# Two copies ahead of two subtractions in a weight fold, and another order of the last projection tiles

## The chip, the cores and the metric

The kernel runs on one core of one Trainium2 chip. The metric is the device time of one execution in microseconds (us), as the median of several runs. A profiled execution stands beside them; its trace gives each instruction's start and duration, and the views of the profile are made from it. Engines are named as the profile does: PE is TensorE (PEld its weight loads), DVE is VectorE, ACT is ScalarE, POOL is GpSimd, SP is SyncE, which issues most transfers.

## What is computed

The reference adds a linear attention with a learned feature map and a two-layer MLP to the input `x` (2048 tokens of width 640, 32 heads of 20, hidden width 1728), both on the layer-normalized input:

```python
xn = layernorm(x)
# attention
qkv = (xn @ wqkv)                       # split into q, k, v per head
pq, pk = q @ w_phi, k @ w_phi           # 20x20 per head
phi_q = concat(softmax(pq), softmax(-pq))
phi_k = concat(softmax(pk), softmax(-pk))
kv  = phi_k^T @ v                       # summed over all tokens, per head
z   = sum over tokens of phi_k
o   = (phi_q @ kv) / (phi_q @ z + 1e-6)
A   = o @ wo
# MLP, on layernorm(xn)
B   = gelu(layernorm(xn) @ w1 + b1) @ w2 + b2
out = x + A + B
```

All of it is float32. The kernel splits each float32 operand into a high and a low part of a shorter format and makes three matmuls of each product (`mm3`, lines 63 to 66: high x high, high x low, low x high). So most of what ACT, DVE and POOL do is such splitting: the high part is a copy, the low part a subtraction of that copy from the source (`split`, lines 51 to 61).

## The kernel before

**Stages.** The tokens lie in four blocks of 512. First PE does the MLP for blocks 0 and 1: 14 chunks of the hidden width in groups `g` of two, for each group and block a first half (width 640 to hidden, five steps of three matmuls for each of two chunks) and a second half (hidden to width, five banks). Then comes the projection of all 16 token tiles of 128 to features and values (`proj`, lines 594 to 603), then the MLP for blocks 2 and 3 with the attention beside it, then the output projection.

**Work beside the MLP.** `mlp.beside` (lines 248 and 290) is a generator that PE's loop moves one step on after every three matmuls. In groups 1 and up for blocks 0 and 1 it is `prep` (line 483): it folds `w_phi` into the key and query weights, makes the statistics of blocks 2 and 3, splits the value weights, and makes the normalized input of blocks 2 and 3.

**The fold.** `prep_fold` (lines 445 to 468) runs for keys and queries and six groups of heads, 12 times. Each time it makes two pieces: four chunks of the width and then one. For a piece, PE makes four matmuls or one into one PSUM bank (line 459; the trace has two entries for each). Of a head's 19 columns 16 go to one place (the main part, `dst`) and 3 to another (the rest, columns from `c3` of `wkv_`). Both are split: copies on ACT (line 55), subtractions on DVE (line 58), all four reading the same bank. Between two pieces lie three steps of PE.

**Who is ordered how.** PE's order is that of the code throughout (line 304). From line 354 to line 568, which holds the fold, ACT, DVE and POOL keep the code's order too. In the projection, behind it, they don't: there a planner at compile time picks the order of ACT, DVE and POOL (and everywhere that of SP's transfers) from a simulated timeline, within what the data allow and what `issue_after` asks for. From group 1 of the second MLP on (line 1014), ACT, DVE and POOL are in the code's order again. The waits that the compiler puts in guard PSUM by bank: in this program two engines don't touch one bank at the same time, even if both read.

**The projection.** Each token tile `t` has four banks `i`: `(t, 0)` the main part of the keys (512 columns), `(t, 1)` the rest of keys and queries and half of the values (492), `(t, 2)` the other values (340), `(t, 3)` the main part of the queries (512). Lines 706 and 707 list their order: up to tile 12 in turn, then a list written out by hand. Banks are taken in turn from three (`ptile`, line 574), by `proj` and by the key sums alike, so a bank must be read out before the third allocation behind it.

`k_tile` (line 642), behind `(t, 1)`, makes the key features: maxima and minima (DVE, L625 and L626), differences (POOL, L636), exponential (ACT, L637), sums and reciprocal (DVE, L639 and L645), multiplication (POOL, L647), then the split into `ft` (ACT L55, DVE L58); all tiles share one buffer for `ft`. `q_tile` (line 678), behind `(t, 3)`, does the like for the queries, with L686 and L688 on POOL and transposes on DVE (L694). `v_parts` (line 653) copies and subtracts the values, first all copies (ACT, L660), then all subtractions (DVE, L662). `kv_tile` (line 664), the key sum, adds a tile's features times values to five banks that stay open; it needs both parts of `ft` and all of the tile's values. It runs two tiles late, behind `(t + 2, 0)`; for tile 14 it stands behind `(15, 2)`, and for tile 15 behind the first half of the next MLP's first group (lines 776 to 786).

Of the kernel before, what the change touches and what calls it, by code (L numbers as in the profile page):

```python
# [10 lines left out]
AF = mybir.ActivationFunctionType  # L11
ALU = mybir.AluOpType
# [28 lines left out]
def f(ap):  # L41
    return ap.bitcast(F32)
# [3 lines left out]
def tile_kernel(ctx: ExitStack, tc: tile.TileContext, x, xT, wkT, wqT, wv, wphi, wo, w1, b1, w2, b2,  # L46
                ident, mmask, emask, vsel, out):
    nc = tc.nc
    ctx.enter_context(nc.allow_low_precision(reason="float32 operands are split exactly into float32r parts"))

    def split(hi, lo, src, scale=None, eng=nc.vector, first=nc.scalar):

        if scale is None:
            if first is nc.scalar:
                nc.scalar.activation(hi, src, AF.Copy)  # L55
            else:
                first.tensor_copy(hi, src)
            eng.tensor_tensor(lo, src, f(hi), op=ALU.subtract)  # L58
        else:
            nc.scalar.activation(hi, src, AF.Copy, scale=scale)  # L60
            nc.vector.scalar_tensor_tensor(lo, src, scale, f(hi), op0=ALU.mult, op1=ALU.subtract)
# [371 lines left out]
    wkv_ = [kvw.tile([P, KC, CB[2]], F32R, name=f"wk{p}") for p in "hl"]  # L433
# [11 lines left out]
    def prep_fold(n, g, raw):  # L445


        kk, kd = (G6, G5) if g < 5 else (2 * DH, 2 * DF)
        nh = kd // DF
        c3 = F1 + (F2 if n == "q" else 0) + 18 * g  # L450
        if n == "k":
            dst = [w[:, :, 96 * g:96 * g + 16 * nh] for w in wkv_]
        else:
            t = fp.tile([P, 2, KC, G5], F32R, name="t").rearrange("p a c f -> p a (c f)")[:, :, :KC * 16 * nh]
            dst = [t[:, p].rearrange("p (c q) -> p c q", c=KC) for p in range(2)]
        for k, ni in ((0, 4), (4, 1)):
            ps = mlp.px()
            for i in range(ni):
                nc.tensor.matmul(ps[:, i * kd:(i + 1) * kd], raw[:kk, (k + i) * P:(k + i + 1) * P],  # L459
                                 wpt[:kk, g, :nh, 1:], start=True, stop=True)  # L460
            src = ps[:, :ni * kd].rearrange("p (i h f) -> p i h f", i=ni, f=DF)
            split(*[w[:, k:k + ni].rearrange("p c (h f) -> p c h f", f=16) for w in dst], src[:, :, :, 0:16])
            split(*[w[:, k:k + ni, c3:c3 + 3 * nh].rearrange("p c (h f) -> p c h f", f=3) for w in wkv_], src[:, :, :, 16:])
            for _ in range(3):
                yield
        if n == "q":
            for p in range(2):
                nc.sync.dma_start(wq_dram[p][:, :, 96 * g:96 * g + 16 * nh], f(dst[p]))
# [14 lines left out]
    def prep():  # L483
# [6 lines left out]
        for i, job in enumerate(jobs):  # L490
            raw = ahead
            ahead = raws(*jobs[i + 1]) if i < 11 else None
            for k, _ in enumerate(prep_fold(*job, raw)):
                if i > 0 and k % 2:
                    next(more, None)
                yield
# [97 lines left out]
    def proj(t, i):  # L594

        yh, yl = y[t // 4]
        c = slice((t % 4) * P, (t % 4) * P + P)
        c0 = CB[i - 1] if i else 0
        wh, wl = [w[:, :, c0:CB[i]] for w in wkv_] if i < 3 else wq_
        ps = ptile()[:, :wh.shape[2]]  # L600
        for kc in range(KC):
            mm3(ps, yh[:, kc, c], yl[:, kc, c], wh[:, kc], wl[:, kc], kc == 0, kc == KC - 1)
        return ps
# [11 lines left out]
    def evacuate(ps, n, c):  # L615

        p3 = pks[n].rearrange("p (h f) -> p h f", f=DH)
        return nc.scalar.activation(p3[:, :, c], ps.rearrange("p (h f) -> p h f", h=H), AF.Copy).ins  # L618
# [23 lines left out]
    def k_tile(t):  # L642
        e, sm = features(t, "k")
        w = kp.tile([P, 2 * H], F32, name="w")
        nc.vector.reciprocal(w, sm)  # L645
        e3 = e.rearrange("p s (h f) -> p (s h) f", f=DH)
        nc.gpsimd.tensor_tensor(e3, e3, w.unsqueeze(2).to_broadcast([P, 2 * H, DH]), op=ALU.mult)  # L647
        ft = wp.tile([P, 4, D], F32R, name="w1")
        fh, fl = ft[:, 0:2], ft[:, 2:4]
        split(fh, fl, e)  # L650
        return ft

    def v_parts(t, *parts):

        v = vbuf[t % 2].rearrange("p (g c) -> p g c", c=VS)
        rs = rs_all[:, t:t + 1]
        parts = [(ps.rearrange("p (g c) -> p g c", g=n), v[:, g0:g0 + n, 3:3 + w], v[:, g0:g0 + n, 67:67 + w])
                 for ps, g0, n, w in parts]
        for src, hi, lo in parts:
            nc.scalar.activation(hi, src, AF.Copy, scale=rs)  # L660
        for src, hi, lo in parts:
            nc.vector.scalar_tensor_tensor(lo, src, rs, f(hi), op0=ALU.mult, op1=ALU.subtract)  # L662
# [15 lines left out]
    def q_tile(t):  # L678


        e, sm = features(t, "q")
        w = kp.tile([P, 2 * H], F32, name="w")
        nc.vector.reciprocal(w, sm)
        e = e.rearrange("p s f -> p (s f)")
        for (hs, sv), (_, wv_), (_, ev) in zip(by_head(sm, 1), by_head(w, 1), by_head(e, DH)):
            nc.gpsimd.tensor_tensor(wv_[:, 1], sv[:, 0], wv_[:, 1], op=ALU.mult)  # L686
            shape = list(ev[:, 1].shape)
            nc.gpsimd.tensor_tensor(ev[:, 1], ev[:, 1], wv_[:, 1].to_broadcast(shape), op=ALU.mult)  # L688

        b, i = divmod(t, 4)  # L690
        if i == 0:
            ets[b] = [places[n % 5] for n in range(4 * b, 4 * b + 4)]
        for n, et in enumerate(ets[b]):
            nc.vector.transpose(et[:, :, 32 * i:32 * i + 32], e[:, 320 * n:320 * n + 320].rearrange("p (j r) -> p j r", r=32))  # L694

    def store_phi(b, n):

        ed = e_dram[b][320 * n:320 * n + 320, :].rearrange("(j r) (q n) -> q r j n", r=32, q=4)
        for q in range(4):
            nc.sync.dma_start(ed[q], ets[b][n][32 * q:32 * q + 32])  # L700
# [2 lines left out]
    places = [acc01.tile([P, KC, 512], F32, name=f"acc{n}").rearrange("p c (j n) -> p (c j) n", n=P) for n in range(2)]  # L703
    places = [p[:, j:j + 10] for p in places for j in (0, 10)] + [et.tile([P, 10, P], F32, name="et")]

    for t, i in [(t, i) for t in range(13) for i in range(4)] + [(13, 0), (13, 1), (13, 2), (14, 0), (14, 1), (13, 3), (15, 0), (15, 1),
                                                                  (14, 3), (15, 3), (14, 2), (15, 2)]:
        if (t, i) in ((4, 0), (8, 0)):
            b = t // 4 + 1
            y[b] = [yp.tile([P, KC, 512], F32R, name=f"y{p}{b % 2}") for p in range(2)]  # L710
            for p in range(2):
                nc.sync.dma_start(f(y[b][p]), y_dram[b - 2][p])
        ps = proj(t, i)
        pq = 1 + t % 3
        if i == 0:
            evac = evacuate(ps, 0, slice(1, 17))
        elif i == 1:
            evac = evacuate(ps[:, :F2], 0, slice(17, 20))
            evacuate(ps[:, F2:2 * F2], pq, slice(17, 20))
            v_parts(t, (ps[:, 2 * F2:], 0, 5, G3))  # L720
            fts[t] = k_tile(t)
        elif i == 2:
            v_parts(t, (ps[:, :15 * DH], 5, 5, G3), (ps[:, 15 * DH:17 * DH], 10, 1, 2 * DH))
        else:
            evac = evacuate(ps, pq, slice(1, 17))
            q_tile(t)

        tk = 14 if (t, i) == (15, 2) else t - 2 if t > 1 and i == 0 else None
        if tk is not None:
            kv_tile(tk, fts.pop(tk), vbuf[tk % 2])  # L730
        if t and t % 4 == 0:
            store_phi(t // 4 - 1, i)
        if i == 0 and t in (1, 2, 3, 6, 7):

            kc = (1, 2, 3, 6, 7).index(t)
            lo = rp.tile([P, D], F32, name="r1")
            hi = rp.tile([P, D], F32R, name="r2")
            nc.sync.dma_start(lo, wo[kc * P:(kc + 1) * P, :])
            with tc.issue_after(evac):
                split(hi, lo.bitcast(F32R), lo, eng=nc.gpsimd)  # L740
            for w, wd in zip((f(hi), lo), wo_dram):
                nc.sync.dma_start(wd[:, kc, :], w)
        if (t, i) == (11, 0):
            mlp = Mlp((0, 2, 3, 1), ((1, 2), (0, 3)))
            mlp.ph = ptile
            mlp.fetch(0)
        if (t, i) == (12, 3):
            with tc.issue_after(evac):
                ws = [mlp.take(0)]
            mlp.fetch(1)  # L750
        if (t, i) == (15, 3):
            w, late = mlp.take_parts(1)
            ws.append(w)
            late.pop(0)()
# [248 lines left out]
    for g in range(7):  # L1003
        for b in range(2, 4):
# [23 lines left out]
            if (g, b) == (0, 3):  # L1028
# [5 lines left out]
                op = ctx.enter_context(tc.tile_pool(name="oB", bufs=1, reuse_waits="tile"))  # L1034
# [83 lines left out]
```

## Time and profile before

| what | us |
|---|---|
| median of 3 runs (738.99 to 740.37) | 739.7 |
| profiled execution | 739.42 |
| its span, first to last instruction | 737.6 |
| PE busy | 721.1 |
| DVE busy | 480.2 |
| POOL busy | 368.6 |
| ACT busy | 324.3 |

The mean granted clock of PE is 0.997 of full speed. A row of the timeline reads: start, duration, engine, line of the kernel, operation, written tile and read tiles, shape, count; in brackets the idle time of the engine before it and what ended that. A row of the waits reads: the engine and line that waited, what it waited for, us in total, times, longest. A row of the windows reads: the stretch and its length, then for PE, PEld, DVE, ACT and POOL the busy time and number of instructions, then the granted clock, the share of the DMA engines and GB/s.

### The profile page before, as it was taken

To read this page: it belongs to the slowest core of one execution; us is meant where nothing else is said; L and a number is where in the kernel's file an instruction comes from. 1 tells how busy PE (TensorE), PEld (TensorE's weight loads), DVE (VectorE), ACT (ScalarE), POOL (GpSimd) and SP (SyncE) were. 2 spreads that over 40 slices of the span, in tenths; PEclk is the share of its full clock that TensorE was granted. 3 is DMA by queue.
4 is the path that set the end of the run, shared out by engine and by line. 5 is a ranking of instruction groups with operands and counts; after the bars stand their busy time and mean duration, and the time that the engine had idled before them with its cause. 6 is when DMAs were issued, how large, how long until landed. Compare 5 with 4: busy or idle time off the path is not lost.

```text
span 737.6 us, 9732 instructions
## 1 busy us (share of the span) xinstructions
PE 721.1 (98%) x3440; PEld 603.5 (82%) x3440; DVE 480.2 (65%) x811; ACT 324.3 (44%) x550; POOL 368.6 (50%) x322
## 2 busy tenths in 40 slices
PE   9999999899999999999999998999999999999998
PEld 7787788688888888888888887888878888877887
DVE  7836754657643888888878787535575656767331
ACT  7624354343322555454355456246555556440110
POOL 2210212344411797797787889246576777304000
PEclk9999999999999999999999999999999999999999
DMA  9604465555433124634600706843433343154222
GB/s 328 210 19 122 146 167 143 199 201 171 152 144 143 59 84 161 161 95 156 143 1 0 179 1 204 207 131 110 126 115 111 117 154 92 48 208 131 85 82 75
DMA packets 65832, 95.55 MB, mean 130 GB/s; under 512 B 14624, under 2 KB 36528, under 8 KB 64160
## 3 DMA queue, kind: packets, MB, share of 16 engines
q1 hardware_dynamic: 65496, 94.92, 41.4%
q8 instruction: 27, 0.44, 0.3%
q14 instruction: 21, 0.17, 0.1%
q10 hardware_dynamic: 288, 0.01, 0.0%
HBM read 64.56 MB, written 30.35 MB: 129 GB/s over the span
## 4 chain that ended last, share of the span: by engine, by line
PE 87%; DVE 7%; DMA 3%; ACT 2%; issue 1%; SPq 0%; DVEq 0%; ACTq 0%
PE bank L64 26%; PE bank L66 25%; PE bank L65 25%; PE bank L667 2%; PE bank L459 2%; PE bank L889 1%; PE bank L888 1%; DVE st L130 1%; DMA raw<-in_wv 1%; DVE y L953 1%; DMA t<-in_x 1%; PE bank L274 1%; PE bank L273 1%; PE bank L824 1%; DVE y L58 0%
## 5 line engine op out<-in xcount | busy, mean ns | idle before, releaser
L58 POOL TENSOR_TENSOR w<-r,w 128x640 fp32r<-128x640 f32 x52 | 83.5, 1622 | 109.1 <-ACT w L55 75.6
L64 PE MATMUL bank<-y,w 128*128 128x512 f32 (+1 forms) x334 | 130.9, 392 | 0.4 <-DVE ob L1057 0.4
L66 PE MATMUL bank<-y,w 128*128 128x512 f32 (+1 forms) x334 | 129.8, 389 | 0.0
L65 PE MATMUL bank<-y,w 128*128 128x512 f32 (+1 forms) x334 | 129.7, 388 | 0.0
L64 PE MATMUL bank<-m,w 128*128 128x512 f32 x260 | 104.7, 403 | 7.6 <-DVE acc L297 5.1
L66 PE MATMUL bank<-m,w 128*128 128x512 f32 x260 | 102.3, 394 | 0.0
L65 PE MATMUL bank<-m,w 128*128 128x512 f32 x260 | 102.0, 392 | 0.0
L297 DVE TENSOR_TENSOR acc<-bank,acc 128x512 f32<-128x512 f32 x120 | 80.3, 682 | 16.1 <-PE bank L66 10.4
L64 PE MATMUL bank<-wkh,y 128*128 128x512 f32 (+2 forms) x240 | 87.5, 365 | 0.0
L66 PE MATMUL bank<-wkh,y 128*128 128x512 f32 (+2 forms) x240 | 87.0, 363 | 0.0
L65 PE MATMUL bank<-wkl,y 128*128 128x512 f32 (+2 forms) x240 | 87.0, 363 | 0.0
L58 DVE TENSOR_TENSOR m<-m,m 128x512 fp32r<-128x512 f32 (+1 forms) x54 | 44.0, 815 | 56.4 <-ACT m L55 56.4
L64 PEld LDWEIGHTS bank<-y,w 128*128 128x128 f32 x334 | 62.8, 188 | 13.5 <-DVE ob L1057 0.8
L66 PEld LDWEIGHTS bank<-y,w 128*128 128x128 f32 x334 | 62.7, 188 | 12.9
L65 PEld LDWEIGHTS bank<-y,w 128*128 128x128 f32 x334 | 62.9, 188 | 12.7
L64 PEld LDWEIGHTS bank<-m,w 128*128 128x128 f32 x260 | 49.2, 189 | 21.6 <-DVE acc L297 7.8
L636 POOL TENSOR_TENSOR m<-m,mx 128x640 f32<-128x640 f32 (+2 forms) x48 | 43.1, 912 | 43.6 <-DVE mx L625 43.6
L618 ACT ACTIVATE m<-bank 128x512 f32<-128x512 f32 (+1 forms) x64 | 26.4, 439 | 86.3 <-PE bank L66 60.6
L882 POOL TENSOR_TENSOR e<-e,m 120x512 fp32r<-120x512 f32 (+1 forms) x28 | 37.9, 1357 | 43.9 <-ACT m L881 43.3
L252 ACT ACTIVATE m<-bank,b1t 128x512 f32<-128x512 f32 (+1 forms) x54 | 36.2, 670 | 50.6 <-PE bank L66 44.9
L639 DVE TENSOR_REDUCE sm<-m 128x64 f32<-128x1280 f32 x32 | 47.3, 1478 | 17.0 <-ACT m L637 16.8
L66 PEld LDWEIGHTS bank<-m,w 128*128 128x128 f32 x260 | 49.0, 188 | 10.5
(158 smaller groups left out, 1416.5 us busy)
## 6 DMA issues: line engine op xcount, KB each, us to landing
r<-in_w SPq DMA_DIRECT2D x52, 320.0 KB
e<-e SPq DMA_DIRECT2D x40, 240.0 KB
e<-acc SPq DMA_DIRECT2D x52, 160.0 KB
acc<-in_xT SPq DMA_DIRECT2D x4, 1280.0 KB
xb<-in_x SPq DMA_DIRECT2D x8, 320.0 KB
t<-in_x SPq DMA_DIRECT2D x8, 320.0 KB
raw<-in_xT SPq DMA_DIRECT2D x10, 256.0 KB
yh<-t SPq DMA_DIRECT2D x10, 256.0 KB
```

Source lines behind the costliest of these rows:

```text
L58: eng.tensor_tensor(lo, src, f(hi), op=ALU.subtract)
L64: nc.tensor.matmul(ps, lh, rh, start=first, stop=False, **kw)
L65: nc.tensor.matmul(ps, lh, rl, start=False, stop=False, **kw)
L66: nc.tensor.matmul(ps, ll, rh, start=False, stop=last, **kw)
L252: nc.scalar.activation(gt, pz, AF.Gelu_apprx_tanh, bias=b1t[:, 2 * g + j:2 * g + j + 1])
L297: nc.vector.tensor_tensor(acc[b][:, m, :], pw, acc[b][:, m, :], op=ALU.add)
L459: nc.tensor.matmul(ps[:, i * kd:(i + 1) * kd], raw[:kk, (k + i) * P:(k + i + 1) * P], wpt[:kk, g, :nh, 1:], start=True, stop=True)
L618: return nc.scalar.activation(p3[:, :, c], ps.rearrange("p (h f) -> p h f", h=H), AF.Copy).ins
L636: subs[n, t] = nc.gpsimd.tensor_tensor(ep[:, s], a, b, op=ALU.subtract)
L639: nc.vector.tensor_reduce(sm, e.rearrange("p s (h f) -> p (s h) f", f=DH), axis=AX, op=ALU.add)
L667: nc.tensor.matmul(kvp[g // 2][:VM, (g % 2) * 240:(g % 2) * 240 + 240].rearrange("p (s f) -> p s f", s=4), v[:, g * VS:g * VS + VM], ft[:, ...
L882: nc.gpsimd.tensor_tensor(pl, e, f(ph), op=ALU.subtract)
```

## The change

In `prep_fold`, both copies of a piece are issued first and then both subtractions; before, main copy, main subtraction, rest copy and rest subtraction followed each other. In the list of the last projection tiles, `(14, 2)` goes from behind `(15, 3)` to behind `(13, 3)`. The key sum of tile 14 goes from behind `(15, 2)` to behind `(14, 3)`. The hand-written part of PE's order is so:

```
before: 13.0 sum11 13.1 13.2 14.0 sum12 14.1 13.3 15.0 sum13 15.1 14.3 15.3 14.2 15.2 sum14
after:  13.0 sum11 13.1 13.2 14.0 sum12 14.1 13.3 14.2 15.0 sum13 15.1 14.3 sum14 15.3 15.2
```

```diff
@@ -459,8 +459,13 @@
                 nc.tensor.matmul(ps[:, i * kd:(i + 1) * kd], raw[:kk, (k + i) * P:(k + i + 1) * P],
                                  wpt[:kk, g, :nh, 1:], start=True, stop=True)
             src = ps[:, :ni * kd].rearrange("p (i h f) -> p i h f", i=ni, f=DF)
-            split(*[w[:, k:k + ni].rearrange("p c (h f) -> p c h f", f=16) for w in dst], src[:, :, :, 0:16])
-            split(*[w[:, k:k + ni, c3:c3 + 3 * nh].rearrange("p c (h f) -> p c h f", f=3) for w in wkv_], src[:, :, :, 16:])
+            main = [w[:, k:k + ni].rearrange("p c (h f) -> p c h f", f=16) for w in dst]
+            rest = [w[:, k:k + ni, c3:c3 + 3 * nh].rearrange("p c (h f) -> p c h f", f=3) for w in wkv_]
+            both = [(*main, src[:, :, :, 0:16]), (*rest, src[:, :, :, 16:])]
+            for hi, _, z in both:
+                nc.scalar.activation(hi, z, AF.Copy)
+            for hi, lo, z in both:
+                nc.vector.tensor_tensor(lo, z, f(hi), op=ALU.subtract)
             for _ in range(3):
                 yield
         if n == "q":
@@ -703,8 +708,8 @@
     places = [acc01.tile([P, KC, 512], F32, name=f"acc{n}").rearrange("p c (j n) -> p (c j) n", n=P) for n in range(2)]
     places = [p[:, j:j + 10] for p in places for j in (0, 10)] + [et.tile([P, 10, P], F32, name="et")]
 
-    for t, i in [(t, i) for t in range(13) for i in range(4)] + [(13, 0), (13, 1), (13, 2), (14, 0), (14, 1), (13, 3), (15, 0), (15, 1),
-                                                                  (14, 3), (15, 3), (14, 2), (15, 2)]:
+    for t, i in [(t, i) for t in range(13) for i in range(4)] + [(13, 0), (13, 1), (13, 2), (14, 0), (14, 1), (13, 3), (14, 2), (15, 0), (15, 1),
+                                                                  (14, 3), (15, 3), (15, 2)]:
         if (t, i) in ((4, 0), (8, 0)):
             b = t // 4 + 1
             y[b] = [yp.tile([P, KC, 512], F32R, name=f"y{p}{b % 2}") for p in range(2)]
@@ -725,7 +730,7 @@
             evac = evacuate(ps, pq, slice(1, 17))
             q_tile(t)
 
-        tk = 14 if (t, i) == (15, 2) else t - 2 if t > 1 and i == 0 else None
+        tk = 14 if (t, i) == (14, 3) else t - 2 if t > 1 and i == 0 else None
         if tk is not None:
             kv_tile(tk, fts.pop(tk), vbuf[tk % 2])
         if t and t % 4 == 0:
```

## The prediction

> **What bounds the kernel now.** I read the page's busy times first.
>
> ```profile
> span 737.6 us, 9732 instructions
> PE 721.1 (98%) x3440; PEld 603.5 (82%) x3440; DVE 480.2 (65%) x811; ACT 324.3 (44%) x550; POOL 368.6 (50%) x322
> ```
>
> TensorE (PE) is the bound; no other engine passes 65%. The change takes no matmul away, so it can win only idle time of PE, 737.6 - 721.1 = 16.5 us in all, or clock. The next view is who PE waited for, and beside it the two rows of all waits that the fold's edit is about (us in total, times, longest).
>
> ```profile
> PE bank L64 <- DVE acc L297: 5.1, 4, 1.8
> PE bank L64 <- DVE acc L295: 2.5, 3, 1.1
> PE bank L667 <- DVE w L58: 1.9, 2, 1.4
> PE bank L667 <- DVE v L662: 1.4, 1, 1.4
> ...
> ACT wkh L55 <- DVE wkl L58: 17.6, 12, 3.0
> ACT wkh L55 <- DVE t L58: 6.3, 12, 0.8
> ```
>
> The fold's second copy stood 17.6 + 6.3 = 23.9 us, in all 24 pieces, behind a subtraction whose result it doesn't read. That is ACT's time and not PE's: PE pays only where an eviction (L295, L297) comes late. The first two rows of PE are such places, the last two are in the tail of the projection. The timeline of PE says where in the fold:
>
> ```profile
> 67.23 0.50 PE L64 MATMUL bank<-m,w 128*128 128x512 f32 x1 [0.74 <-DVE acc L295]
> 69.97 0.47 PE L64 MATMUL bank<-m,w 128*128 128x512 f32 x1 [1.08 <-DVE acc L295]
> ...
> 72.34 0.39 PE L64 MATMUL bank<-m,w 128*128 128x512 f32 x1
> ...
> 77.25 0.50 PE L64 MATMUL bank<-m,w 128*128 128x512 f32 x1 [1.78 <-DVE acc L297]
> ...
> 81.18 0.45 PE L64 MATMUL bank<-m,w 128*128 128x512 f32 x1
> ...
> 139.18 0.50 PE L64 MATMUL bank<-m,w 128*128 128x512 f32 x1 [1.50 <-DVE acc L297]
> ```
>
> The first three stalls make 3.60 us within 11 us; the last one belongs to a later part. Then the clock: 77.25 to 81.18 holds the same fourteen matmuls (six of 512 columns, eight of the fold) as 69.97 to 72.34, and takes 3.93 us against 2.37, 1.56 more. The view by windows (the granted clock is the third number from the right) shows why:
>
> ```profile
> 79.00:81.00 2.00, 2.00 (x9) 1.81 (x8) 1.29 (x4) 0.49 (x1) 0.00 (x0) 0.50 0.59 182
> ...
> 139.00:141.00 2.00, 1.66 (x6) 1.05 (x6) 0.86 (x2) 1.51 (x3) 0.00 (x0) 1.00 0.37 120
> ```
>
> **The fold's edit.** It removes no instruction and, on each engine, changes no order: ACT still does main copy, rest copy, and VectorE (DVE) main subtraction, rest subtraction. What changes is who waits: the rest copy no longer for the main subtraction, but the main subtraction now for the rest copy, some 0.23 us. Behind it on DVE stand the rest subtraction, the statistics and the evictions, for which PE waits. ACT and DVE in the stretch:
>
> ```profile
> 70.02 0.19 ACT L55 ACTIVATE wkh<-bank 128x18 fp32r<-128x18 f32 x1 [1.97 <-DVE wkl L58]
> 70.22 1.28 ACT L143 ACT_TABLE_LOAD   x1
> 71.51 0.21 ACT L143 ACTIVATE sr<-q 128x8 f32<-128x8 f32 x1
> 71.63 1.35 ACT L55 ACTIVATE w<-r 128x640 fp32r<-128x640 f32 x2
> ```
> ```profile
> 65.43 0.89 DVE L130 BATCH_NORM_STATS2 st<-t 128x6 f32<-128x320 f32 x2 [0.91 <-DMA t<-in_x]
> ...
> 67.93 0.23 DVE L58 TENSOR_TENSOR wkl<-bank,wkh 128x72 fp32r<-128x72 f32 x1 [0.30 <-ACT wkh L55]
> 69.12 0.70 DVE L295 SCALAR_TENSOR_TENSOR acc<-bank,b2t,acc 128x512 f32<-128x512 f32 x1
> 70.47 0.74 DVE L295 SCALAR_TENSOR_TENSOR acc<-bank,b2t,acc 128x512 f32<-128x512 f32 x1
> 71.75 0.20 DVE L144 RECIPROCAL rr<-sr 128x8 f32<-128x8 f32 x1 [0.54 <-ACT sr L143]
> 73.39 0.56 DVE L58 TENSOR_TENSOR wkl<-bank,wkh 128x384 fp32r<-128x384 f32 x1 [0.18 <-ACT wkh L55]
> 76.56 0.64 DVE L297 TENSOR_TENSOR acc<-bank,acc 128x512 f32<-128x512 f32 x1
> ```
>
> Step by step. **Stall 1** (0.74) hangs on DVE's wait for a load of x at 65.43; it stays. **Stall 2**: DVE's 0.30 at 67.93 goes, since both copies are long done when it gets there; the eviction of 69.12 comes 0.3 sooner: 0.3 won. **Stall 3** ends with the eviction of 76.56 + 0.64. Its chain goes back through ACT: the rest copy at 70.02 had waited 1.97, and only behind it could the square root's table load start (1.28). With the rest copy straight behind its main copy, load and all are done before DVE has the root's input (some 70.0, as two waits of 0.30 and 0.25 ahead of it go). The root is then at 70.0 for 71.51. The reciprocal of 71.75 is held by the eviction in front of it, 70.47 + 0.74 = 71.21 less 0.6, so it starts at 70.6, 1.15 sooner. ACT's two weight copies start near 70.2 for 71.63, the next fold's main copy after them near 71.5 (its matmuls end about there), its rest copy by 72.2, and DVE's subtraction at 72.25 for 73.39. Another 0.30 between the two subtractions goes, and the eviction of 76.56 comes at 75.1. PE resumes at 75.8 for 77.25: **1.45 won**, stall 2's 0.3 among it, with 0.6 of the third stall left. **Clock**: it stayed 1.00 behind the stall of 1.50 at 139 and fell only behind 1.78 with two more shortly before; with 0.6 in its place I take the whole 1.56 as won. Fold: 1.45 + 1.56 = **3.0**.
>
> Bounds: at best stalls 2 and 3 and the clock go, 1.08 + 1.78 + 1.56 = 4.4. At worst the new wait costs DVE 0.23 in each of the three pieces ahead of a stall and nothing else moves, 0.7 lost; the removed 0.30 on the same path speaks against a loss, so I keep 0 to 4.4. Behind 82 us PE has no wait to 139 and the transfers there are issued as PE goes, so the gain should travel on.
>
> The row says that a copy waited for a subtraction of other columns. The Trainium skill, "PSUM — Partial Sum Buffer", section "PSUM bank collisions raise a hardware error", says why such a wait must be there: two engines may not touch one bank and quadrant at once, reads against reads included. By that rule the edit can't remove the waiting, only turn it round, as I counted it. The trace agrees, with 24 such waits.
>
> **The tail of the projection.** The same fifteen matmuls of (14,2) go from behind (15,3) to behind (13,3), with two copies and two subtractions for its values; tile 14's key sum (eleven matmuls and one addition of 0.27 us) goes from behind (15,2) to behind (14,3). No transfer moves, and none is issued by these steps. PE:
>
> ```profile
> 438.01 0.39 PE L64 MATMUL bank<-w,y 128*128 128x512 f32 x1
> ...
> 439.37 0.32 PE L64 MATMUL bank<-wkh,y 128*128 128x340 f32 x1
> ...
> 443.96 0.72 PE L667 MATMUL bank<-w,v 128*127 128x240 f32 x5
> 446.05 0.83 PE L667 MATMUL bank<-w,v 128*127 128x240 f32 x5 [1.37 <-DVE v L662]
> ```
> ```profile
> 432.81 0.40 ACT L618 ACTIVATE m<-bank 128x96 f32<-128x96 f32 x2 [1.08 <-PE bank L66]
> ```
> ```profile
> 435.08 1.60 DVE L58 TENSOR_TENSOR w<-m,w 128x1280 fp32r<-128x1280 f32 x1
> 436.61 0.52 DVE L662 SCALAR_TENSOR_TENSOR v<-bank,rs_all,v 128x300 fp32r<-128x300 f32 x1
> 445.49 1.28 DVE L662 SCALAR_TENSOR_TENSOR v<-bank,rs_all,v 128x300 fp32r<-128x300 f32 x4
> 453.70 1.49 DVE L58 TENSOR_TENSOR w<-m,w 128x1280 fp32r<-128x1280 f32 x1 [1.42 <-ACT w L55]
> ```
> ```profile
> 430.35 2.37 POOL L647 TENSOR_TENSOR m<-m,w 128x1280 f32<-128x1280 f32 x1
> ...
> 443.82 1.43 POOL L636 TENSOR_TENSOR m<-m,mx 128x600 f32<-128x600 f32 x2
> 449.32 2.37 POOL L647 TENSOR_TENSOR m<-m,w 128x1280 f32<-128x1280 f32 x1
> ```
>
> (14,2) and (15,2) take (443.96 - 439.37)/2 = 2.3 us each, a bank of 512 columns 5 x (439.37 - 438.01)/2 = 3.4. Times here are those of before, without the fold's gain.
>
> Key sum 14 waited 1.37 us for values copied only at 445.49. After, PE comes to it at 443.96 - 2.3 - 3.4 = 438.3; its values are then over ten us old, and its features are ready at 435.08 + 1.60 = 436.7: **1.37 won**. What is late next? The banks turn by three, and (15,3) now takes (15,1)'s. That was read last at 436.61 + 0.52, 4.3 us behind its end (432.81); it now ends 2.3 later, so 439.4, and PE is there at 438.3 + 1.3 = 439.6 (1.3 for a key sum, from 0.72 and 0.83 less what overlaps). That is no margin, and tile 13's transposes may get in front on DVE: I charge 0.4.
>
> Key sum 15 waited 1.40 (the longest of the waits of L667 for DVE w), until 453.70 + 1.49 = 455.19. PE was there at 453.8 and now comes at 453.8 - 1.37 + 0.4 = 452.9. From POOL's multiplication (449.32) to that end went 5.9 us, so it must start by 447.0. Tile 15's keys leave PE 2.3 later, at 435.1. Tile 14's went from bank to this multiplication in 8.9 us (421.46, quoted next, to 430.35): that gives 444.0, at most 2.8 more for a pair of query subtractions in front, 446.8.
>
> ```profile
> 421.46 0.40 ACT L618 ACTIVATE m<-bank 128x96 f32<-128x96 f32 x2 [4.41 <-PE bank L66]
> ```
>
> So it is in time: **1.40 won**. But tile 15 itself took 449.32 - 432.81 = 16.5 before, because POOL did query 15's subtractions (443.82) and more first. By that lag it starts at 451.6, 2.3 later than before, and so does the end. POOL's order here is made by the planner at compile time and I can't read it from the trace. I take tile 14's lag, because query 15 leaves PE 3.9 later than before and keys 15 only 2.3, which favours the keys. Bounds of the tail: 2.8 won, 3.9 lost (below). Taken: 1.37 + 1.40 - 0.4 = **2.4**.
>
> **Sum.** 3.0 + 2.4 = 5.4. The profiled execution took 739.42 (span 737.6 and 1.8 around it), 0.3 under the median of 739.7: 734.0 for it, and **734.3** for the median.
>
> **Rivals.** *The wait moves to key sum 15*: keys 15 keep the lag of 16.5 us. For it: POOL was busy without a gap there and did query 15 first. Against: the new order of PE. Tail +2.3: 739.7 - 3.0 + 2.3 = 739.0; with POOL a little quicker, down to 736.7 (tail nothing).
>
> *The clock still falls*: 734.3 + 1.6 = 735.9. For it: 0.74 + 0.78 + 0.6 = 2.1 us of stalls stay close together. Against: 1.50 us at 139 did not bring it down. The Trainium skill, "TensorE: Matmul & The Clock Gate", section "Part 1: The HAM clock gate", has the clock fall after an idle window of about 3.4 us. By that rule a gap of 1.78 isn't the cause and shortening it wins no clock; the trace disagrees so far as it fell to 0.50 with no gap longer than 1.78.
>
> *Slower*: POOL keeps keys 15's multiplication behind query 15's subtractions, which now start 3.9 later. It starts at 453.2 and the key sum ends 3.9 later than before; with the fold at half, 1.5, that is 739.7 - 1.5 + 3.9 = 742.1, with all of the fold 740.6. It decides from a start at 449.3 + 1.5 + the fold's gain: 452.3 with half, 453.8 with all of it.
>
> *The fold's edit does nothing for PE*, as all three stalls hang on loads of x: 739.7 - 2.4 = 737.3.
>
> **How the numbers follow.** Forecast 40%, wait moved to key sum 15 25% (half of it within 0.2%), clock still down 20%, slower 8% (5 beyond 0.2%), fold without effect 7%. 0.2% is 1.5 us, about what a measurement of this kernel can tell from no change. Faster 40 + 12 + 20 + 7 = 79%, the same 13 + 3 = 16%, slower 5%. The range goes from the fold's best, 739.7 - 4.4 - 2.4 = 732.9, to 739.2, just past the moved wait; it leaves out the rival on the other side.
>
> **What would show it.** Right: the waits of the second copy for a subtraction gone; a table load near 67 to 69 and PE resuming near 75.8; clock 1.00 to 83; key sum 14 without a wait, key sum 15 without one. Wrong: a stall of over 1.5 near 75, clock 0.50 behind it; a wait of 2 us or more ahead of key sum 15, with POOL's L647 behind a pair of L636 on 600 elements; a new wait at (15,3).

## The result, and the profile after

| | before | after |
|---|---|---|
| median | 739.35 (738.65 to 740.37, 4 runs) | 734.57 (734.34 to 734.82, 4 runs) |
| profiled execution | 739.42 | 734.51 |
| its span | 737.6 | 732.7 |

The ratio of after to before is 0.9934, 95% interval 0.9917 to 0.9952: 4.8 us faster. Forecast were 5.4 and, from a median of 739.7 before, a time of 734.3.

The page's busy times after, and the waits of PE (engine and line that waited, what for, us in total, times, longest):

```profile
span 732.7 us, 9756 instructions
PE 718.9 (98%) x3440; PEld 601.5 (82%) x3440; DVE 478.6 (65%) x811; ACT 322.6 (44%) x550; POOL 368.3 (50%) x322
```
```profile
PE bank L64 <- DVE acc L297: 3.8, 4, 1.5
PE bank L64 <- DVE acc L295: 1.9, 3, 0.7
PE bank L64 <- ACT m L252: 1.2, 1, 1.2
PE bank L672 <- DVE w L58: 0.5, 1, 0.5
```

PE's busy time fell by 2.2 us for the same 3440 matmuls; a matmul lasts longer at a low clock (fourteen of them, below, took 3.93 us at 0.50 and 2.39 at 1.00), so that part can't come from waits. In the waits, L297 went from 5.1 to 3.8 and L295 from 2.5 to 1.9 (the fold), both waits of the tail are gone (what is left of L672, five lines further down than L667, is one of 0.5 at an earlier tile), and a row is new: 1.2 us for ACT's L252, the gelu of the MLP.

To see where the time went, I compare the start of the same matmul of PE in both traces, after minus before. The points are times of before:

| at | 68.5 | 75.1 | 77.8 | 81.5 | 126.8 | 424 | 457.7 | 469 | end |
|---|---|---|---|---|---|---|---|---|---|
| after | -0.24 | -0.64 | -1.88 | -3.47 | -3.51 | -3.37 | -5.13 | -4.84 | -4.82 |

So the fold gave 3.47 by 81.5 and the tail 1.47 from 424 to 469, while some 0.1 was lost on the way. The fold, in the timeline of PE after (start, us; in brackets the idle time and what ended it):

```profile
66.98 0.50 PE L64 MATMUL bank<-m,w 128*128 128x512 f32 x1 [0.54 <-DVE acc L295]
69.33 0.47 PE L64 MATMUL bank<-m,w 128*128 128x512 f32 x1 [0.69 <-DVE acc L295]
75.38 0.50 PE L64 MATMUL bank<-m,w 128*128 128x512 f32 x1 [0.55 <-DVE acc L297]
77.77 0.39 PE L64 MATMUL bank<-m,w 128*128 128x512 f32 x1
```

The three stalls are now 0.54, 0.69 and 0.55. The matmul at 77.77 is the one that stood at 81.18: 75.38 to 77.77 is 2.39 for the fourteen matmuls that took 3.93. The windows say the same by the clock (third number from the right):

```profile
77.00:79.00 2.00, 2.00 (x11) 1.66 (x11) 0.67 (x3) 0.61 (x2) 0.00 (x0) 1.00 0.71 236
79.00:81.00 2.00, 2.00 (x12) 1.67 (x11) 1.97 (x6) 1.44 (x4) 0.41 (x1) 1.00 0.29 35
```

ACT shows the mechanism:

```profile
66.48 0.33 ACT L466 ACTIVATE wkh<-bank 128x96 fp32r<-128x96 f32 x2 [1.69 <-PE bank L459]
66.83 1.28 ACT L143 ACT_TABLE_LOAD   x1
69.61 0.21 ACT L143 ACTIVATE sr<-q 128x8 f32<-128x8 f32 x1 [1.50 <-DVE q L138]
```

Both copies of the one-chunk piece are one entry of two, and the table load follows at 66.83, 3.39 before its place of old (70.22). ACT then waits 1.50 for the root's input: the load is off the path, and the root comes at 69.61 for 71.51.

The tail, first POOL, then ACT:

```profile
439.96 2.37 POOL L652 TENSOR_TENSOR m<-m,w 128x1280 f32<-128x1280 f32 x1 [0.35 <-DVE w L650]
442.29 1.58 POOL L58 TENSOR_TENSOR w<-r,w 128x640 fp32r<-128x640 f32 x1
443.82 1.42 POOL L641 TENSOR_TENSOR m<-m,mx 128x600 f32<-128x600 f32 x2
445.20 2.67 POOL L641 TENSOR_TENSOR m<-mx,m 128x600 f32<-128x600 f32 x2
```
```profile
447.90 1.37 ACT L642 ACTIVATE m<-m,rs_all 128x1280 f32<-128x1280 f32 x1 [3.25 <-POOL m L641]
449.29 1.28 ACT L252 ACT_TABLE_LOAD   x1
450.58 1.27 ACT L252 ACTIVATE m<-bank,b1t 128x512 f32<-128x512 f32 x2
```
```profile
451.32 0.50 PE L64 MATMUL bank<-y,w 128*128 128x512 f32 x1 [1.24 <-ACT m L252]
```

Tile 15's multiplication (L652) now runs ahead of query 15's differences (L641, 443.82), as the forecast chose. What is late next is a chain behind these differences: they end at 447.87, then come query 15's exponential (L642), the load of the gelu's table and the gelu (L252), which reads out a bank of the next MLP. PE wants that bank back and waits 1.24 us. The second pair of these differences took 2.67, where before it took 1.43 (POOL L636 at 445.20); DVE's split of tile 15's features (445.40 to 447.75) now runs beside it.

### The profile page after: what moved, and what is told of

It reads as the page before. It is cut to its first block, busy times and chain, and to the rows that moved or that the text cites. A ratio compares the mean times of both kernels' runs of the same rounds, so it can differ in the third digit from the quotient of the medians.

```text
span 732.7 us, 9756 instructions
## 1 busy us (share of the span) xinstructions
PE 718.9 (98%) x3440; PEld 601.5 (82%) x3440; DVE 478.6 (65%) x811; ACT 322.6 (44%) x550; POOL 368.3 (50%) x322
## 4 chain that ended last, share of the span: by engine, by line
PE 83%; DVE 8%; ACT 2%; POOL 2%; DMA 2%; issue 2%; SPq 0%; DVEq 0%; POOLq 0%; ACTq 0%
PE bank L64 25%; PE bank L65 24%; PE bank L66 24%; PE bank L672 2%; PE bank L459 2%; PE bank L894 1%; PE bank L893 1%; DMA raw<-in_wv 1%; DVE st L130 1%; DVE y L958 1%; POOL m L652 1%; POOL m L641 1%; PE bank L274 1%; PE bank L273 1%; DVE sm L644 1%
## 5 line engine op out<-in xcount | busy, mean ns | idle before, releaser
L297 DVE TENSOR_TENSOR acc<-bank,acc 128x512 f32<-128x512 f32 x120 | 80.8, 683 | 17.3 <-PE bank L66 11.4
L64 PEld LDWEIGHTS bank<-m,w 128*128 128x128 f32 x260 | 48.9, 188 | 19.7 <-DVE acc L297 6.8
L641 POOL TENSOR_TENSOR m<-m,mx 128x640 f32<-128x640 f32 (+2 forms) x48 | 43.1, 912 | 42.8 <-DVE mx L630 42.8
L252 ACT ACTIVATE m<-bank,b1t 128x512 f32<-128x512 f32 (+1 forms) x54 | 36.1, 671 | 53.2 <-PE bank L66 47.4
L66 PEld LDWEIGHTS bank<-m,w 128*128 128x128 f32 x260 | 48.8, 188 | 10.4
L65 PEld LDWEIGHTS bank<-m,w 128*128 128x128 f32 x260 | 49.0, 188 | 10.0 <-DVE m L58 0.4
```

The lines of the kernel that those rows point to most:

```text
L64: nc.tensor.matmul(ps, lh, rh, start=first, stop=False, **kw)
L65: nc.tensor.matmul(ps, lh, rl, start=False, stop=False, **kw)
L66: nc.tensor.matmul(ps, ll, rh, start=False, stop=last, **kw)
L252: nc.scalar.activation(gt, pz, AF.Gelu_apprx_tanh, bias=b1t[:, 2 * g + j:2 * g + j + 1])
L297: nc.vector.tensor_tensor(acc[b][:, m, :], pw, acc[b][:, m, :], op=ALU.add)
L641: subs[n, t] = nc.gpsimd.tensor_tensor(ep[:, s], a, b, op=ALU.subtract)
```

## The experiments

Medians stand beside those of the kernel before, run with them on the same chip: 739.31 for e1 to e4, 739.51 for e5, e6, e8 and e9, 739.36 for e10, e11 and e13. A ratio is that of the kernel to this one, with its 95% interval.

**e1: the fold alone**, with the old list of tiles and the old place of key sum 14.

```diff
-[..., (13, 3), (14, 2), (15, 0), (15, 1), (14, 3), (15, 3), (15, 2)]
+[..., (13, 3), (15, 0), (15, 1), (14, 3), (15, 3), (14, 2), (15, 2)]
-        tk = 14 if (t, i) == (14, 3) else ...
+        tk = 14 if (t, i) == (15, 2) else ...
```

> The fold's edit alone, with the tile order and the key sum of before. Theory: the fold gave 3.4 us of the 4.8 (PE's stall at 139.2 us of before stands at 135.7 after): 735.9 us, clock 1.00 to 83 us, stalls of 0.5 to 0.7 at 67, 69 and 75, and the two tail waits of 1.4 as before. Rival, the split of the prediction (3.0 for the fold): 736.3. Rival, that the tail of before swallows some of the fold's gain: 737 or more, with a tail wait over 1.6.

736.60, ratio 0.9963 (0.9951 to 0.9975): 2.7 won, less than the 3.4 of the theory and nearer to the rival's 3.0; the trace gains 3.0. The matmul of 81.5 comes 3.24 sooner, and that holds to 424; in the tail both old waits are there, key sum 14's a little longer as PE comes to it sooner:

```profile
443.03 0.83 PE L672 MATMUL bank<-w,v 128*127 128x240 f32 x5 [1.59 <-DVE v L667]
```

**e2: the tail alone**, with the old fold.

```diff
-            for hi, _, z in both:
-                nc.scalar.activation(hi, z, AF.Copy)
-            for hi, lo, z in both:
-                nc.vector.tensor_tensor(lo, z, f(hi), op=ALU.subtract)
+            for piece in both:
+                split(*piece)
```

> The tile order and the early key sum alone, with the fold of before. Theory: two waits of 1.37 and 1.40 go and one of 1.24 for a bank that gelu reads late comes in: 1.5 won, 737.8 us, the clock at 0.5 to 0.7 from 77 to 81 us. Rival, the prediction's 2.4: 736.9. Rival, that the planner's order without the fold's edit is another and the wait moves to key sum 15: 739 or more.

738.62, ratio 0.9986 (0.9978 to 0.9995): 0.7 won for 1.5 expected; the trace gains 1.1. From 424 to 469 the trace gains 1.6, with the new wait for the gelu in it (1.25); 0.65 was lost between 127 and 198, where the edit changes nothing. The two parts alone make 3.4 of the 4.8 that they make together; in the traces they make 3.0 and 1.1, and the difference is in e1's longer wait and in that place of e2.

**e3: the fold's edit for key groups 2 and 3 only**, the folds around the three stalls, with the old tail.

```diff
+            for together in ([both] if n == "k" and g in (2, 3) else [[p] for p in both]):
-            for hi, _, z in both:
+                for hi, _, z in together:
...
-            for hi, lo, z in both:
+                for hi, lo, z in together:
```

> Copies first in the third and fourth of the twelve folds alone (key groups 2 and 3), the other ten and the tail as before. Theory: only these stand on the path of the three stalls, so nearly all of the fold's gain is there: 735.9 to 736.4 us. Rival, the gain is spread over all 24 pieces: 3.4 x 4/24 = 0.6, so 738.8.

737.32, ratio 0.9976 (0.9966 to 0.9986), later than the theory's 736.4 and far from the rival's 738.8. At 81.5 it has won as much as e1 (3.15), but at 126.8 only 1.69 is left. Between the two a stall stands that neither before nor after has:

```profile
85.65 0.50 PE L66 MATMUL bank<-y,w 128*128 128x512 f32 x1 [0.64 <-DVE rr L145]
```

ACT's copies behind the two folds stand again behind subtractions:

```profile
80.87 0.37 ACT L467 ACTIVATE wkh<-bank 128x72 fp32r<-128x72 f32 x2 [2.80 <-DVE wkl L469]
83.15 0.19 ACT L467 ACTIVATE wkh<-bank 128x18 fp32r<-128x18 f32 x1 [1.91 <-DVE wkl L469]
83.23 1.36 ACT L55 ACTIVATE w<-r 128x640 fp32r<-128x640 f32 x2
```

The high parts of the MLP's weights (L55) wait in that queue; POOL makes the low parts from them, and PE's matmul at 85.65 loads a low part (the row names L145 on DVE; the semaphore that its weight load waits for is POOL's, and in the trace of after DVE's L145 ends at 84.66, behind this matmul's start at 84.47). The stall is 0.64 of the 1.46 lost; the rest goes in smaller delays up to 107, which weren't followed. e1, which differs from e3 by the ten other folds alone, loses nothing there. So PE coming sooner needs the next folds sooner too: the edit's gain is kept by the other folds.

**e6: the edit for one piece only**, the one-chunk piece of key group 2, whose rest copy stood at 70.02 ahead of the root's table load (the condition of e3 becomes `(n, g, k) == ("k", 2, 4)`).

> Copies first in a single piece of the 24, the one-chunk piece of the third fold, whose second copy stands ahead of the table load; everything else as before. Theory: the load and the square root come 1.1 to 1.4 us sooner, so the third stall falls from 1.78 to some 0.6 to 0.8 with the second still at 1.08, and the clock stays at 1.00: 2.5 us won at 82 us of the trace; of that up to 1.5 may be lost again behind the other folds, as with the third and fourth alone: 736.8 to 738.2 us. Rival, the two stalls are made by the waits of 0.30 on VectorE and not by the load: 0.3 us won, clock at 0.5 behind 77 us, 739.0.

738.90, ratio 0.9991 (0.9982 to 1.0001), with a spread of 737.7 to 740.1: the median misses the expected 736.8 to 738.2 and can't be told from no change. The profiled execution (737.88) has the third stall at 0.54, the second unchanged at 1.09, the clock at 1.00, and is 2.86 sooner at 81.5; 1.0 of that is gone by 126.8, as in e3:

```profile
69.94 0.47 PE L64 MATMUL bank<-m,w 128*128 128x512 f32 x1 [1.09 <-DVE acc L295]
75.98 0.50 PE L64 MATMUL bank<-m,w 128*128 128x512 f32 x1 [0.54 <-DVE acc L297]
85.70 0.50 PE L66 MATMUL bank<-y,w 128*128 128x512 f32 x1 [0.47 <-DVE rr L145]
```

In the trace one copy of 24 carries the third stall, so the theory of the table load holds there. Why the median keeps less than the profiled execution stays open; the clock isn't the reason, as eight of the ten runs have a mean clock of 0.999 or 1.000 and still lie between 737.71 and 740.00.

**e4: the new wait taken away.** The changed kernel with the low part of chunk 1's `w1` made on DVE in place of POOL, which takes 1.58 us (442.29) from ahead of query 15's differences.

```diff
-        def take_parts(self, c):
+        def take_parts(self, c, eng=nc.gpsimd):
...
-                lambda: split(w1h, w1l, r1, eng=nc.gpsimd),
+                lambda: split(w1h, w1l, r1, eng=eng),
...
-            w, late = mlp.take_parts(1)
+            w, late = mlp.take_parts(1, nc.vector)
```

> The changed kernel, with one subtraction (first weight of the second chunk, 1.58 us on GpSimd ahead of query 15's differences) moved to VectorE. Theory: the new wait of 1.24 at 451.3 us is gelu waiting behind query 15's exponential, which waits for GpSimd; 1.5 less in front of it removes the wait: 733.4 us. Rival, the wait is set by the table load or by PE itself: 734.6, with a wait of over 0.8 still there.

733.52, ratio 0.9925 (0.9914 to 0.9937): 1.05 under the changed kernel's median, the lowest here. The changed kernel was run apart from it, and the intervals of the two ratios overlap; the spans of the traces, 731.4 for 732.7, differ by 1.3. The differences start at 442.17, the wait is 0.31:

```profile
450.26 0.51 PE L64 MATMUL bank<-y,w 128*128 128x512 f32 x1 [0.31 <-ACT m L252]
```

**e5: the early key sum undone.** The changed kernel with tile 14's keys summed behind (15, 2) again.

```diff
-        tk = 14 if (t, i) == (14, 3) else ...
+        tk = 14 if (t, i) == (15, 2) else ...
```

> The changed kernel with tile 14's key sum back behind (15, 2); the tile order stays. The planner then puts tile 15's multiplication on GpSimd behind query 15's differences, the second weight's subtraction and a memset, and its first copy on ScalarE behind both gelus. Theory: the wait moves to key sum 15, as the prediction's rival had it: about 4 us there instead of none, the gelu wait of 1.24 gone, so some 3 us over the changed kernel: 737.6 us. Rival, that moving the sum buys nothing beside the tile order: 734.6.

741.06, ratio 1.0026 (1.0015 to 1.0037): slower than before, and 3.5 over the expected 737.6. The planner turned POOL's order: tile 15's multiplication stands behind query 15's differences and a memset, and key sum 15 waits 5.53 us for the expected 4, behind which the clock is at 0.50, which the theory hadn't counted:

```profile
441.39 1.42 POOL L641 TENSOR_TENSOR m<-m,mx 128x600 f32<-128x600 f32 x2
442.77 1.42 POOL L641 TENSOR_TENSOR m<-mx,m 128x600 f32<-128x600 f32 x2
444.15 1.57 POOL L58 TENSOR_TENSOR w<-r,w 128x640 fp32r<-128x640 f32 x1
445.66 1.28 POOL L809 MEMSET kvs<- 120x1408 f32 x1
446.89 2.38 POOL L652 TENSOR_TENSOR m<-m,w 128x1280 f32<-128x1280 f32 x1
```
```profile
454.36 2.49 PE L672 MATMUL bank<-w,v 128*127 128x240 f32 x10 [5.53 <-DVE w L58]
```
```profile
456.00:458.00 2.00, 2.00 (x8) 1.81 (x8) 1.62 (x2) 2.00 (x5) 2.00 (x2) 0.50 0.02 4
```

**e13: that order put back, the sum left late.** e5, with query 15's differences asked to follow tile 15's multiplication.

```diff
...
-                subs[n, t] = nc.gpsimd.tensor_tensor(ep[:, s], a, b, op=ALU.subtract)
+                with tc.issue_after(muls[15].ins) if (n, t) == ("q", 15) else ExitStack():
+                    subs[n, t] = nc.gpsimd.tensor_tensor(ep[:, s], a, b, op=ALU.subtract)
...
-        nc.gpsimd.tensor_tensor(e3, e3, w.unsqueeze(2).to_broadcast([P, 2 * H, DH]), op=ALU.mult)
+        muls[t] = nc.gpsimd.tensor_tensor(e3, e3, w.unsqueeze(2).to_broadcast([P, 2 * H, DH]), op=ALU.mult)
```

> The kernel of e5 (tile 14's key sum behind the last bank again) with query 15's differences on POOL made to stand behind key tile 15's multiplication. In e5 POOL did them first, PE waited 5.53 us at key sum 15, and the clock fell behind that. Theory, the loss is POOL's order alone, which the planner turns when the sum comes late: key sum 14 ends near 442, the features of tile 15 are written near 447 as in the changed kernel, no wait at key sum 15, clock 1.00, 734.6. Rival, the late sum itself is what costs, since both tiles share the buffer of the features: a wait of over 2 us stays at key sum 15, 737 or more.

735.10 (734.07 to 737.85, 4 runs; the last has a mean clock of 0.995), ratio 0.9945 (0.9926 to 0.9963). The profiled execution, 734.07, has no wait at either key sum and only the gelu's wait, as after:

```profile
440.60 1.28 PE L673 MATMUL bank<-w,v 128*127 128x240 f32 x10
...
448.64 1.28 PE L673 MATMUL bank<-w,v 128*127 128x240 f32 x10
```
```profile
441.36 2.36 POOL L653 TENSOR_TENSOR m<-m,w 128x1280 f32<-128x1280 f32 x1
443.69 1.20 POOL L642 TENSOR_TENSOR m<-m,mx 128x600 f32<-128x600 f32 x1
```

So the late sum costs nothing that can be seen here by itself; what the early sum bought was the order that the planner picks. e5's loss is POOL's order, with the fall of the clock that followed from the wait.

**e8 to e11: the clock.** The changed kernel with halves of the statistics made more than once (the result stays the same); tile 12's stand on DVE ahead of the third stall's eviction, tile 10's and 11's ahead of the first and second.

```diff
-            for h in range(2):
+            for h in [0, 1] + ([0, 1, 0][:3] if t == 12 else []):         # e8
+            for h in [0, 1] + ([0, 1, 0][:2] if t == 12 else []):         # e9
+            for h in [0, 1] + ([0, 1] if t in (10, 11, 12) else []):      # e10
+            for h in [0, 1] + ([0, 1] * 3 if t == 12 else []):            # e11
```

> The changed kernel with three extra half-row statistics of tile 12 on VectorE (0.44 us each, same results), ahead of the eviction that ends the third stall: that stall grows from 0.55 by 1.3 to about 1.85. Theory, the clock falls with the length of that stall: 0.5 behind it for some 3.4 us, 1.3 + 1.55 = 2.9 us over the changed kernel, 737.4. Rival, the clock's fall before came of something else in the old fold: 1.3 alone, 735.9, clock 1.00.

> The same with two extra halves: the third stall grows by 0.9 to about 1.43. Theory, that a stall of this length (1.50 at 139 us kept the clock at 1.00) does not bring the clock down: 0.9 us over the changed kernel, 735.5, clock 1.00. Rival, the sum of the stalls within a few us decides and not the last one: clock at 0.5, 737.0.

> The changed kernel with each half of the statistics of tiles 10, 11 and 12 made twice (no result changes). Each extra half showed 0.39 us of stall where three stood ahead of stall 3 (0.55 to 1.73). Two more ahead of each stall give 0.54 + 0.8 = 1.3, 0.69 + 0.8 = 1.5 and 0.55 + 0.8 = 1.3, together 4.1 us within 10 us, more than the 3.60 of the kernel before, but none as long as its 1.78. Theory A, the clock goes by how much PE idles in such a stretch: granted clock 0.50 behind the third stall, 734.6 + 2.3 + 1.5 = 738.4, in most executions. Theory B, it goes by the length of a single stall, from some 1.7 up: clock 1.00, 736.9.

> The changed kernel with the halves of tile 12's statistics made four times: six extra halves ahead of stall 3 alone, 0.55 + 6 x 0.39 = 2.9, stalls 1 and 2 as they were (0.54, 0.69), together the same 4.1 us. Theories A and B both say that the clock falls: 738.4. If a single gap must pass 3.4 us or so, the clock stays at 1.00 and the time is 736.9. Together with the run before it: falls in both, A; falls here alone, B; in neither, the longer gap.

| kernel | median (range, runs) | stalls in the trace | clock behind them | runs with a mean clock of 0.998 or less |
|---|---|---|---|---|
| after | 734.57 (734.34 to 734.82, 4) | 0.54, 0.69, 0.55 | 1.00 | 0 of 4 |
| e9 | 735.91 (735.02 to 737.87, 4) | 0.66, 0.69, 1.33 | 1.00 | 1 of 4 |
| e8 | 736.05 (735.81 to 737.74, 6) | 0.68, 0.70, 1.73 | 1.00 | 2 of 6 |
| e10 | 737.23 (737.03 to 737.44, 5) | 1.47, 1.47, 1.33 | 1.00 | 0 of 5 |
| e11 | 738.51 (736.41 to 739.61, 12) | 0.69, 0.69, 2.90 | 0.50 | 11 of 12 |
| e2 | 738.62 (737.39 to 739.21, 11) | 0.56, 1.07, 1.79 | 0.50 | 8 of 11 |
| before | 739.31 to 739.51 (58) | 0.74, 1.08, 1.78 | 0.50 | 29 of 58 |

The stalls are from the profiled execution of each, the last column from all runs: a stretch of 3.4 us at half the clock, 1.7 in 737, shows as 0.998 in the mean over the span. That column counts a fall anywhere. Of three kernels with stalls like those of after, e1 shows a low mean in 0 of 5 runs, e4 in 1 of 6 and e13 in 1 of 4, so the counts of e9 and e8 can't be told from theirs. The ratios to before are 0.9954 (0.9937 to 0.9971) for e9, 0.9959 (0.9946 to 0.9971) for e8, 0.9968 (0.9956 to 0.998) for e10 and 0.9983 (0.9974 to 0.9992) for e11. The third stall and the windows behind it, of e8, of e10 and of e11:

```profile
76.83 0.50 PE L64 MATMUL bank<-m,w 128*128 128x512 f32 x1 [1.73 <-DVE acc L297]
```
```profile
77.00:79.00 2.00, 2.00 (x14) 1.78 (x15) 1.58 (x5) 0.28 (x1) 0.00 (x0) 1.00 0.66 183
```
```profile
77.91 0.50 PE L64 MATMUL bank<-m,w 128*128 128x512 f32 x1 [1.33 <-DVE acc L297]
```
```profile
80.00:82.00 2.00, 2.00 (x11) 1.66 (x11) 1.42 (x4) 0.40 (x2) 0.00 (x0) 1.00 0.53 161
```
```profile
78.10 0.50 PE L64 MATMUL bank<-m,w 128*128 128x512 f32 x1 [2.90 <-DVE acc L297]
```
```profile
80.00:82.00 2.00, 2.00 (x8) 1.71 (x8) 1.73 (x5) 0.61 (x2) 0.00 (x0) 0.50 0.56 164
```

e8's theory missed: the clock held behind 1.73 in the trace, and the median is the rival's. e10 and e11 have the same 4.3 us of stalls within some 11 us. In e10, split in three, no run has a low mean clock; in e11, with one long stall, the mean clock is low in all but one. So idle time doesn't add up over such a stretch. At 1.78 (before, and e2 with the same fold) one execution falls and the next doesn't. Length alone doesn't decide it either: behind a later stall of 2.03 at 140.57 e11's clock stayed at 1.00.

The traces say more than the runs were made for. The granted clock is 0.50 from 77.88 to 81.29 in before, from 78.15 to 81.57 in e2 and from 78.98 to 82.40 in e11, 3.4 us each, and from 452.94 to 459.77 in e5, twice that. Each of the four traces has one more fall, behind the last matmul, and the starts of the two falls lie 658.77, 658.77, 658.78 and 286.72 us apart: 193, 193, 193 and 84 times 3.413. So the clock changes on a grid of 3.41 us, which lies elsewhere in each execution. In the step of that grid ahead of its fall PE idled 1.78 (before), 1.79 (e2), 2.53 (e11) and 3.41 (e5). All thirteen traces have that last fall, so the grid can be laid back from it in each. No other step ahead of the last matmul then has more than 1.75 us of idle PE, but for one of 1.88 in e11, where the border cuts the stall of 2.03; behind these the clock held. The steps ahead of the thirteen last falls have 1.98 or more. My reading, which no run was made to test, is that the clock falls when PE idles for some half of one step or more; as 1.78 fell and 1.88 held, the line isn't sharp in this count. By it a stall of 1.78 has to lie whole in a step. That gives, as an estimate, (3.41 - 1.78) / 3.41 = 48% of executions, and 29 of 58 showed a low mean clock.

## Why the prediction was right, and where it was wrong

**What bounds it, and which waits.** Right: the gain came from idle time of PE and from the clock in the stretch and in the tail that the rows of PE's waits had named.

**Fold, forecast 3.0.** Right in mechanism and nearly in size. Stall 2 went from 1.08 to 0.69 (0.78 forecast), stall 3 from 1.78 to 0.55 (0.6 forecast), the clock gave 1.54 (3.93 less 2.39; 1.56 forecast). PE resumed at 75.38 for 75.8 forecast. e6's trace shows that stall 3 went by the chain that the prediction followed, the rest copy ahead of the table load. The bound below, a loss of 0.7 by DVE's new wait, was far off: stalls 2 and 3 got shorter. The first stall, which the forecast left as it was, says nothing on this: it was 0.74 before and 0.54 after, but 0.56 in e2 with the old fold and 0.71 in e13 with the new one. One thing wasn't seen: what the stretch gives is kept only because the folds behind it were changed as well (e3, e6). "Behind 82 us PE has no wait to 139" was read from a PE that came there 3 us later.

**Clock.** The step "it stayed 1.00 behind the stall of 1.50 at 139 and fell only behind 1.78 with two more shortly before" left open whether the length or the neighbours did it. e10 against e11 says that neighbours within 11 us don't, and the grid of 3.41 us in the traces adds where in it the stall lies. The rival *the clock still falls* didn't come: none of the four runs after has a mean clock of 0.998 or less. The price in the median is less sure than in the one execution. In the 29 runs of before with a mean clock of 0.998 or less the time averages 739.94, in the other 29 it is 739.10, 0.84 apart and not 1.56, and e1 gained 2.7 in the median where its trace gained 3.0. So the trace of before that the sum was made on was one with the clock down, as half of the runs were. In other kernels the same two averages lie further apart, 1.1 in e2, 1.5 in e8 and, with a single run on one side, 2.3 in e11. Why the other half of before is not 1.56 faster stays open; there is no trace of such a run. The Trainium skill, "TensorE: Matmul & The Clock Gate", section "Part 1: The HAM clock gate", has the activity watched in free-running windows of about 3.4 us. The grid of 3.41 us in the traces, and that the same kernel falls in one run and not in the next, agree with a window that runs free; that 1.78 can suffice, and 2.90 did in 11 of 12, doesn't agree with a whole idle window as the condition.

**Tail, forecast 2.4, measured 1.47.** Both waits (1.37 and 1.40) went, and tile 15's multiplication started at 439.96; forecast was 444.0 in times of before, 440.6 less the fold's 3.4. The choice of tile 14's lag over tile 15's was right, and the rivals *wait moved to key sum 15* and *slower* didn't come. But e5 is the rival *slower* in the flesh: with the sum left late the planner does put query 15 first. That its 741.06 lies in the 740.6 to 742.1 worked out is partly luck: tile 15's multiplication started at 446.89, 450.3 in times of before, for 453.2 worked out, and PE's 5.4 us at clock 0.50 behind the wait cost some 2.7 that the sum didn't have. The reason given for the order, that query 15 leaves PE later and keys 15 less so, isn't what decided it: e5 has the new order of tiles as well. Within that order of tiles, key sum 14's place decided the planner's choice.

**The step that failed** is "What is late next?" in the tail. It charged 0.4 for (15, 3)'s bank. There was no wait. The subtraction that read (15, 1)'s bank last, and (15, 3)'s first matmul, after:

```profile
433.92 0.52 DVE L667 SCALAR_TENSOR_TENSOR v<-bank,rs_all,v 128x300 fp32r<-128x300 f32 x1
```
```profile
436.14 0.43 PE L64 MATMUL bank<-w,y 128*128 128x512 f32 x1
```

The bank was free at 434.44, 1.7 us before PE came. And the step looked no further than the key sums. With both waits gone PE comes 2.8 sooner to the first banks of the next MLP, whose gelu stands behind query 15's exponential and so behind POOL's differences of query 15; these start at 443.82 in both traces, though query 14's differences ahead of them came 2.7 sooner (439.54 before, 436.82 after), as POOL now does tile 15's multiplication (2.37, and 0.35 of waiting for it) in between. They also end 1.24 later than before (447.87 for 446.63), by the 2.67 of their second pair. PE waits 1.24, and 1.37 + 1.40 - 1.24 = 1.53 is the tail's 1.47 within 0.1. e4 took most of this wait away (1.24 to 0.31), and its median is 1.05 lower. Whether it would be gone without the slower pair wasn't tried.

The two errors of the sum, 0.5 too little in the fold and 0.9 too much in the tail, cancel in part, and the 739.7 that it was taken from is 0.35 over the median of four runs; that 734.3 came so near to 734.57 is partly luck.

## What to carry to other kernels

When a wait goes, follow the engine that is let go to its *next* claim on every shared buffer, in the next stage too, and ask whether the engine that frees it was moved as well; here the answer lay 2 us behind the end of the stage that was changed. Where a planner sets the order, an edit acts through the order that it picks: moving one sum won because it turned two instructions on POOL, and saying that order outright did as well (e13). Where a profiled execution shows a low clock, look at the mean clock of the other runs before its whole price goes into a median.

## What the runs showed that wasn't expected

- Behind a stall of 2.90 us PE's clock was at 0.50 in the trace, and 11 of that kernel's 12 runs have a mean clock of 0.998 or less; with one of 1.78 or 1.79 it is 29 of 58 and 8 of 11 runs, with three of 1.33 to 1.47 within 11 us none of 5. In the traces the clock falls on a grid of 3.41 us.
- A table load on ACT doesn't wait for the input of the instruction that it is for: it ran at 66.83, and ACT waited 1.50 behind it. A queue that reaches such a load early hides its 1.28.
- Tile 15's features split on DVE took 2.35 us for 128x1280 beside POOL at work, where the same line and shape took 1.53 in e5:

```profile
445.40 2.35 DVE L58 TENSOR_TENSOR w<-m,w 128x1280 fp32r<-128x1280 f32 x1
```
```profile
452.77 1.53 DVE L58 TENSOR_TENSOR w<-m,w 128x1280 fp32r<-128x1280 f32 x1
```

POOL works beside both, and in the first case it was slow as well: in e13, where the split took 2.35 too (445.06 to 447.41), POOL's piece of 40 columns beside it took 1.50 (446.02 to 447.52). That the two engines held each other up is likely by these times and wasn't tried.
